# A three-layer chain on one core: the first stage of an f32 kernel in another written order

## The chip, the core and the metric

The kernel runs on one core of a Trainium2 chip. A core has five engines that work side by side, each through a list of its own: TensorE (PE, matmuls), VectorE (DVE), ScalarE (ACT), GpSimd (POOL) and SyncE (SP, which here issues the DMAs). The metric is the device time of one execution in microseconds, and lower is better.

## What is computed

Chunked attention, then a gated layer behind an RMS norm, then a layer with a cosine gate, all in float32. The reference, cut to its core:

```python
# attention: 8 batches x 8 heads, 576 positions in chunks of 64, head size 64
scores = (1 / sqrt(64)) * q_c @ k_c.T
attn = exp(scores - max(scores));  attn = attn / (sum(attn) + 1e-9)
x = (attn @ v_c) as 4608 tokens x 512
# gated layer, 512 -> 1536 -> 512
xn = x / sqrt(mean(x * x) + 1e-6) * rms_g
x = (silu(xn @ w_gate) * (xn @ w_val)) @ w_out
# cosine layer, 512 -> 2048 -> 512
h = x @ w_in
out = (h * cos(h)) @ w_out2
```

Each float32 factor of the large products is split into two parts of fewer bits, and three matmuls (high by high, high by low, low by high) are added in PSUM.

## The kernel before

The program has four stages. This text is about the first, which ends some 303 us into the span. It does three jobs at once.

**Attention.** The 4608 tokens are 36 units of 128, handled in 18 pairs. For a unit `n` (or pair `u`) the steps have one letter each: `Q` and `V` load q, k and v; `s` multiplies q by k for a pair (L418, for the first pair L401); `m` takes the row maximum on DVE (L435); `b` subtracts it on DVE (L450); `e` is the exponential on ACT (L454); `n` sums on DVE, inverts and scales the row (L459 to L469; for the first two units the scaling is a step `z` of POOL); `t` transposes on PE (L476) and `c` copies the result out on ACT (L481); `v` multiplies by v for a pair (L492); `r` squares and sums on ACT (L506), `w` makes the norm's factor on POOL, `y` applies it on DVE (L517); `x` transposes on PE (L525); `j` rounds the high part on ACT (L534), `a` keeps a full copy on ACT (L539), and `l` makes the low part on DVE (L547; for the first two units on POOL, L545). `X` stores the copy.

**A first third of the gated layer.** Four of the twelve column blocks of `w_gate` and `w_val` are multiplied here in the plain way. The weights of block `f`, matrix `m` (0 gate, 1 value) are loaded by `Dfm` and split by `k`, `p`, `q`, `H`, `L` (ACT, DVE, DVE, ACT, POOL). The tokens go in eleven chunks, `A` to `D` of 256 columns and `E` to `K` of 512. `gA0` is the gate product of chunk A with block 0, 12 matmuls into one PSUM bank, `vA0` the value product; `SA0` is the SiLU on ACT (L594), which empties the gate's bank; `hA0` multiplies the two on DVE (L604), and `Y` stores.

**Preparation of later weights.** Steps `Pl0` to `Pk15` load, split and store sixteen blocks of weights for the second stage.

The gate and value products share a ring of four PSUM banks with the scores of pairs 1 and 3; the other four banks serve scores, transposes and outputs of the attention in turn.

What sets the order: every step is written once in one long table, `ORDER`, and each engine takes its instructions strictly in the order in which the table's steps issue them.

```python
with tc.manual_schedule(engines=FIXED):   # PE, DVE, ACT, POOL, SP
    for name in ORDER.split():
        ...
        step(name)
```

A second table, `ORDER2`, does the same for stages two and three. The steps `O1` and `O2` in the first table already make operands of the second stage, which begins with products named `b` (L293, with 384 columns). Its high parts are casts at L352, its low parts subtractions at L357.

Of the kernel before, what the change touches and what calls it, by code (L numbers as in the profile page):

```python
# [82 lines left out]
def kernel(  # L83
# [58 lines left out]
    a4 = {n: [("op4", n, k) for k in range(2)] for n in range(EARLY4)}  # L142
# [216 lines left out]
    with ExitStack() as st:  # L359
# [290 lines left out]
        def step(name):  # L650
# [16 lines left out]
                units[kind](int(n))  # L667

        ORDER = """
            D00 Q0 k00 Q1 Q2 p00 s0 q00 Q3 H00 I m0 b0 D01 V0 V1 sx m1 Pl0 Dg b1 e0 n0 Q4 e1 L00 z0 s1 n1 t0 m2 b2 Q5 z1 m3  # L670
            t1 V2 b3 e2 c0 c1 k01 e3 v0 n2 n3 t2 r0 t3 Pa0 p01 V3 Pb0 w0 r1 c2 y0 w1 y1 D20 Q6 q01 x0 s2 j0 a0 H01 V4 c3 Pc0
            m4 m5 b4 b5 Pd0 x1 e4 j1 v1 l0 Q7 n4 e5 k20 r2 n5 D21 a1 w2 t4 V5 V6 p20 r3 t5 Pl1 c5 y2 w3 y3 q20 s3 x2 k21 D11
            c4 l1 x3 j2 H20 p21 Q8 v2 m7 m6 gA0 j3 L20 D10 X0 L01 l3 l2 a2 r4 a3 gB0 Pa1 b6 b7 Q9 vA0 q21 e7 n7 vB0 X1 e6 n6
            w4 r5 SA0 w5 t7 H21 k11 SB0 c7 L21 D30 gA2 y4 y5 x4 t6 Pb1 j4 k10 x5 hA0 hB0 l4 a4 a5 p10 j5 Pc1 l5 gB2 s4 V7
            SA2 vA2 vB2 gC2 Ph0 Q10 SB2 Pl2 m9 m8 k30 hA2 b8 Po0 q10 b9 p11 c6 e8 n8 Q11 v3 e9 r7 D31 hB2 n9 p30 q11 gC0 H10
            vC2 t8 SC2 SC0 r6 vC0 w7 L10 YA0 w6 gB1 y7 YB0 YA2 gA1 t9 y6 s5 c8 hC2 hC0 H11 V8 x6 k31 q30 c9 L11 SB1 V9 H30
            Pa2 Q12 X2 vB1 m10 m11 V10 L30 b10 Pk0 vA1 Q13 YB2 YC2 V11 j6 b11 x7 SA1 YC0 v4 a6 p31 Q14 e11 gC1 hA1 Pl3 r9
            e10 q31 r8 H31 hB1 l6 n11 j7 gA3 w9 Pd1 vC1 gB3 w8 L31 n10 a7 SC1 l7 t10 y8 t11 c11 c10 SA3 Ph1 vA3 X3 y9 s6 hC1
            Pb2 x8 Pc2 Po1 x9 SB3 vB3 m12 b12 Q15 Pl4 V12 e12 m13 hA3 b13 hB3 gC3 e13 n12 Pk1 YA1 Pd2 j8 v5 a8 j9 gD1 V13
            Q16 YB1 r10 a9 r11 gD0 l8 V14 t12 SD1 X4 w10 YA3 vD1 n13 l9 y10 c12 x10 SC3 w11 Ph2 t13 y11 hD1 s7 m15 m14 SD0  # L680
            j10 a10 b14 vD0 vC3 c13 l10 e14 x11 v6 gD3 b15 hD0 Q17 gD2 V15 YC1 e15 Po2 r12 a11 Pa4 j11 n14 hC3 n15 w12 Q18
            l11 vD3 r13 w13 t14 SD3 c14 y12 Pb4 y13 vD2 t15 V16 Pc4 s8 x12 c15 SD2 m16 Pa3 j12 x13 m17 b16 gE0 b17 e16 a12
            v7 Q19 vE0 e17 hD3 Pd4 hD2 l12 n16 r14 gE1 Pk2 n17 j13 r15 t16 V17 w15 X5 w14 y15 a13 Ph4 y14 SE0 l13 t17 c17
            Pb3 c16 s9 Po4 m18 b18 gE2 x15 e18 m19 x14 b19 e19 j14 Pc3 Pd3 j15 n19 v8 hE0 r17 a14 V18 X6 w17 SE1 r16 y17 vE1
            vE2 YC3 a15 l15 w16 n18 Pk4 Q20 Q21 hE1 Pl5 Ph3 gE3 y16 t19 V19 l14 V20 Pa5 SE3 c19 SE2 t18 Pb5 s10 m20 X7 hE2
            x16 vE3 Pc5 b20 c18 Po3 m21 b21 x17 gF2 e20 Q22 Pk3 v9 Pd5 Ph5 e21 a16 Pl6 gF0 j16 j17 Po5 n20 r18 l16 r19 n21
            t20 vF0 l17 a17 Pa6 W8 w19 Q23 V21 t21 Pl7 w18 hE3 y19 V22 c20 y18 s11 x18 c21 m22 SF2 SF0 m23 Q24 vF2 Q25 b22
            b23 Pb6 a18 YE1 hF2 Pc6 Pk5 e22 gF3 x19 Pa7 j18 v10 Q26 Pl8 Q27 V23 e23 V24 Pd6 Ph6 YE3 j19 r20 r21 hF0 gF1 n23
            Pb7 w20 l18 Po6 w21 Pc7 SF3 Pa8 SF1 n22 y20 vF3 a19 l19 vF1 t23 c23 t22 y21 Pd7 s12 m25 x20 Pk6 X8 Ph7 c22 a20
            Po7 m24 gG0 b24 x21 b25 j20 a21 e25 Pb8 hF3 v11 e24 r22 j21 V25 Pl9 r23 X9 vG0 Pc8 w23 Pk7 Pa9 n24 hF1 gG2 SG0  # L690
            Pd8 Ph8 y23 Q28 l20 l21 gG1 n25 Pl10 w22 V26 hG0 y22 V27 t24 vG2 YF3 Po8 t25 s13 Pb9 SG2 SG1 Pa10 c24 m27 m26
            b26 YD3 x22 W9 b27 Pc9 c25 j22 a22 Pb10 gG3 Pk8 x23 v12 Pd9 j23 r25 e27 e26 hG2 l23 r24 a23 Pc10 l22 n26 vG1 vG3
            W10 gH2 X10 w24 Q29 w25 SG3 Ph9 Pl11 Po9 Pl12 YF1 n27 W11 y25 t26 c26 t27 y24 s14 hG1 hG3 m28 c27 Pa12 Pb12 b28
            SH2 Q30 YG1 x24 m29 j24 Pd10 e28 gH3 x25 l24 b29 e29 j25 Pk9 V28 Q31 vH2 l25 a24 n28 v13 Q32 YB3 V29 X11 a25 SH3
            r27 r26 w27 w26 Pc12 hH2 n29 gH0 t28 vH3 t29 SH0 Ph10 Po10 c28 Pa11 c29 V30 Q33 y26 y27 s15 x26 gH1 m30 b30 x27
            Pb11 m31 Pk10 hH3 Pc11 b31 a26 j26 j27 vH0 e30 YH3 W12 Pd12 Pl13 YG3 l26 v14 l27 hH0 X12 V31 n30 e31 gI0 r28 r29
            vH1 SH1 Ph12 w28 w29 Po12 n31 t31 y29 a27 Q34 t30 y28 c31 SI0 Pa13 s16 m32 m33 b32 x28 gI2 b33 hH1 Q35 Pk12 Pd11
            c30 W13 x29 j28 SI2 l28 Pb13 gI1 e33 Ph11 Pl14 j29 v15 X13 vI0 Po11 n33 l29 hI0 Pc13 r30 e32 Pk11 r31 a28 SI1
            vI2 Pa14 Pl15 V32 n32 V33 a29 X14 w30 Pd13 t33 gI3 t32 c33 Ph13 c32 YD1 w31 hI2 y30 Pb14 Po13 y31 x30 vI1 Pc14
            s17 hI1 x31 W14 Pk13 V34 vI3 j30 a30 SI3 j31 m34 l30 b34 l31 W19 m35 b35 Pd14 v16 Pa15 hI3 r33 Ph14 gJ2 r32 Po14  # L700
            YD0 W20 YD2 V35 e34 a31 X15 e35 w32 Pb15 W21 Pc15 gJ3 Pk14 SJ2 vJ2 y32 n35 n34 gJ0 t35 t34 Pd15 w33 YH1 y33 c35
            c34 x32 x33 vJ0 SJ3 j32 v17 Ph15 a32 j33 a33 X16 r35 r34 Po15 l32 w34 YI3 w35 vJ3 YI1 hJ2 Pk15 gJ1 hJ3 y34 SJ0
            l33 x34 y35 SJ1 hJ0 j34 x35 j35 a34 vJ1 l35 l34 gK2 gK0 hJ1 a35 X17 Z W15 W16 SK0 SK2 YJ3 vK2 gK1 gK3 W17 W18
            vK0 O1 hK2 hK0 SK3 SK1 vK1 O2 vK3 hK3 hK1 YJ1 YK3 YK1
            """
        nc.gpsimd.memset(mhalf, -0.5)
        nc.gpsimd.memset(halfpi, math.pi / 2)
# [234 lines left out]
    def saved(acc, tag):  # L942
        t = pools["left3"].tile([P, 2, H], F32, tag=tag, name=tag)
        nc.scalar.copy(t, acc)  # L944
        return t
# [248 lines left out]
    with fourth:  # L1194
        for s in range(FIRST, NB):
            for g in range(G3):
                z = {"b1": opened("b1", 2)}
                multiply(z["b1"], s, 1, g, True)
                z1 = saved(z["b1"], "z1")
# [160 lines left out]
```

## Time and profile before

| | |
|---|---|
| time, median of 3 runs | 1626.80 us (1626.78 to 1627.53) |
| the profiled execution | 1626.93 us, of which the span of the program is 1625.1 us |
| PE busy | 1603.0 us, 99% of the span |
| DVE busy | 1362.6 us, 84% |
| ACT busy | 953.4 us, 59% |
| POOL busy | 237.4 us, 15% |

The span is the time from the first to the last instruction on the chip; the 1.8 us between it and the time of that execution lie around it. A matmul's recorded duration is longer than its distance from the next one, since matmuls overlap in the array. So the pace of PE is read from starts of groups, not from durations, and short pauses do not show as idle time. In lists of what the program issues, one f32 matmul of 64 rows stands once (x32), and in the trace it is two passes (x64).

### The profile page before, as it was taken

The numbers are of one execution on the slowest core, as the hardware profiler recorded it, in microseconds if no ns is written. First come the engines' busy times: TensorE is split into PE (matmuls) and PEld (weight loads), VectorE is DVE, ScalarE is ACT, GpSimd is POOL, SyncE is SP. The second block draws the span as 40 slices with busy tenths as digits, with TensorE's granted clock in tenths as the row PEclk, the third lists the DMA queues.
The fourth block names the chain that finished last, engine by engine and source line by source line (L and its number), as shares of the span: only waits on it lengthen the run. The fifth ranks groups of instructions, "written<-read, shape, count | busy, mean of one in ns | idle before, by whom it ended". The sixth has DMA issues, their size and how long they took to land.

```text
span 1625.1 us, 29201 instructions
## 1 busy us (share of the span) xinstructions
PE 1603.0 (99%) x11208; PEld 1556.7 (96%) x11208; DVE 1362.6 (84%) x1862; ACT 953.4 (59%) x1378; POOL 237.4 (15%) x276
## 2 busy tenths in 40 slices
PE   6999999999999999999999999999999999999998
PEld 5998888899999999999999999999999999999998
DVE  7988776588988886889999689988989977877876
ACT  4877665354655544445555478887888634444443
POOL 3434434022223221001112000000000000000000
PEclk9999999999999999999999999999999999999999
DMA  8778988797767778786677864433433665346331
GB/s 294 249 252 277 315 284 270 267 329 247 238 220 250 246 228 272 288 260 201 204 250 243 303 250 145 147 133 130 146 123 120 230 211 163 100 126 185 106 100 39
DMA packets 293131, 342.98 MB, mean 211 GB/s; under 512 B 87936, under 2 KB 265600, under 8 KB 292992
## 3 DMA queue, kind: packets, MB, share of 16 engines
q1 hardware_dynamic: 292192, 341.02, 64.5%
q8 instruction: 88, 1.44, 0.4%
q14 instruction: 51, 0.42, 0.1%
q10 hardware_dynamic: 800, 0.10, 0.0%
HBM read 197.92 MB, written 143.13 MB: 210 GB/s over the span
## 4 chain that ended last, share of the span: by engine, by line
PE 92%; DVE 5%; issue 1%; DMA 0%; ACT 0%; POOL 0%; SPq 0%; DVEq 0%; ACTq 0%; POOLq 0%
PE b L293 76%; PE g L293 6%; PE v L293 6%; PE o L492 1%; PE sc L418 1%; PE tr L525 1%; PE pt L476 1%; DVE xt L357 1%; DVE z L808 1%; DVE wraw L198 0%; DVE z L819 0%; DVE wt L127 0%; DVE wt L128 0%; DMA raw<-in_w_dram 0%; DVE q L339 0%
## 5 line engine op out<-in xcount | busy, mean ns | idle before, releaser
L293 PE MATMUL b<-xo,w 128*128 128x384 f32 x3528 | 612.9, 334 | 0.0
L293 PEld LDWEIGHTS b<-xo,w 128*128 128x128 f32 x3528 | 611.4, 188 | 1.2 <-ACT xo L280 0.7
L293 PE MATMUL b<-xt,w 128*128 128x384 f32 x1728 | 305.9, 335 | 2.4 <-ACT z L804 0.9
L293 PEld LDWEIGHTS b<-xt,w 128*128 128x128 f32 x1728 | 299.6, 188 | 5.2 <-ACT z L804 2.0
L293 PE MATMUL b<-x,w 128*128 128x384 f32 x1440 | 261.9, 334 | 0.2 <-DVE z L808 0.2
L293 PEld LDWEIGHTS b<-x,w 128*128 128x128 f32 x1440 | 250.3, 188 | 1.4 <-DVE z L808 0.6
L280 ACT CAST xo<-q 128x768 fp32r<-128x768 f32 x144 | 118.3, 836 | 117.6 <-PE b L293 97.7
L281 DVE TENSOR_TENSOR xo<-q,xo 128x768 fp32r<-128x768 f32 x144 | 135.2, 953 | 53.2 <-ACT xo L280 53.1
L293 PE MATMUL b<-q,w 128*128 128x384 f32 x864 | 157.7, 334 | 0.0
L293 PEld LDWEIGHTS b<-q,w 128*128 128x128 f32 x864 | 150.5, 188 | 0.0
L251 POOL TENSOR_TENSOR wout<-wt,wout 128x384 fp32r<-128x384 f32 x44 | 54.6, 1242 | 433.2 <-ACT wout L249 330.2
L861 ACT CAST xo<-rawh 128x768 fp32r<-128x768 f32 x98 | 79.7, 836 | 57.6 <-PE b L293 27.8
L804 ACT COPY z<-b 128x768 f32<-128x768 f32 x72 | 57.3, 798 | 88.6 <-PE b L293 64.8
L293 PE MATMUL v<-xt,w 128*128 128x512 f32 (+1 forms) x528 | 107.6, 356 | 0.0
L293 PE MATMUL g<-xt,w 128*128 128x512 f32 (+1 forms) x528 | 107.6, 355 | 0.0
L866 DVE TENSOR_TENSOR xo<-rawh,xo 128x768 fp32r<-128x768 f32 x98 | 96.0, 1013 | 3.2 <-ACT xo L861 3.1
L293 PEld LDWEIGHTS g<-xt,w 128*128 128x128 f32 x528 | 85.7, 189 | 13.3
L293 PEld LDWEIGHTS v<-xt,w 128*128 128x128 f32 x528 | 85.6, 189 | 13.0
L808 DVE TENSOR_TENSOR z<-b,z 128x768 f32<-128x768 f32 x72 | 68.3, 952 | 31.6 <-PE b L293 20.4
L949 DVE TENSOR_TENSOR u<-b,z 128x768 f32<-128x768 f32 x72 | 68.2, 952 | 15.6 <-ACT z L944 12.7
L969 DVE SCALAR_TENSOR_TENSOR q<-q,u 128x768 f32<-128x768 f32 x72 | 68.5, 952 | 10.7 <-ACT q L967 10.2
L959 DVE SCALAR_TENSOR_TENSOR q<-q,u 128x768 f32<-128x768 int32 x72 | 68.2, 952 | 10.0 <-ACT q L955 9.7
(139 smaller groups left out, 2068.2 us busy)
## 6 DMA issues: line engine op xcount, KB each, us to landing
wraw<-in_w_dram SPq DMA_DIRECT2D x240, 128.0 KB, 3.4
gd<-q SPq DMA_DIRECT2D x80, 384.0 KB, 2.5
q<-gd SPq DMA_DIRECT2D x80, 384.0 KB, 3.9
rawh<-hd SPq DMA_DIRECT2D x66, 384.0 KB, 5.4
w<-kout SPq DMA_DIRECT2D x49, 512.0 KB, 7.0
qk<-in_qk_dram SPq DMA_DIRECT2D x36, 512.0 KB, 6.2
kgv<-wout SPq DMA_DIRECT2D x16, 896.0 KB, 6.5
w<-kgv SPq DMA_DIRECT2D x28, 512.0 KB, 6.7
```

The lines of the kernel that those rows point to most:

```text
L251: nc.gpsimd.tensor_tensor(b[n][:, :, 1], a, f32(b[n][:, :, 0]), op=ALU.subtract)
L280: nc.scalar.copy(hi, a)
L281: nc.vector.tensor_tensor(lo, a, f32(hi), op=ALU.subtract)
L293: nc.tensor.matmul(acc, a, b, start=first and k == 0 and q == 0, stop=k == n - 1 and q == 2, skip_group_check=True)
L357: nc.vector.tensor_tensor(o[:, 1], sourceg(s, j), f32(o[:, 0]), op=ALU.subtract)
L804: nc.scalar.copy(sums[s, g, k], z[s, g, "b1"])
L808: nc.vector.tensor_tensor(t, z[s, g, "b2" if k == 0 else "b5"], t, op=ALU.add)
L861: nc.scalar.copy(to[0], source2(s, g, j))
L866: nc.vector.tensor_tensor(to[1], source2(s, g, j), f32(to[0]), op=ALU.subtract)
L949: nc.vector.tensor_tensor(t, acc, part, op=ALU.add)
L959: nc.vector.scalar_tensor_tensor(q, k, -1.0, u, op0=ALU.mult, op1=ALU.add)
L969: nc.vector.scalar_tensor_tensor(q, q, -PI2, u, op0=ALU.add, op1=ALU.mult)
```

## The change

One literal is replaced: the table `ORDER` of the first stage. It has the same steps, each once, in another order; nothing else in the file differs. The steps of one chain keep their order among themselves. Its first two lines were and are:

```diff
         ORDER = """
-            D00 Q0 k00 Q1 Q2 p00 s0 q00 Q3 H00 I m0 b0 D01 V0 V1 sx m1 Pl0 Dg b1 e0 n0 Q4 e1 L00 z0 s1 n1 t0 m2 b2 Q5 z1 m3
-            t1 V2 b3 e2 c0 c1 k01 e3 v0 n2 n3 t2 r0 t3 Pa0 p01 V3 Pb0 w0 r1 c2 y0 w1 y1 D20 Q6 q01 x0 s2 j0 a0 H01 V4 c3 Pc0
...
+            D00 Q0 Q1 k00 Q2 p00 q00 s0 m0 I Q3 b0 e0 sx m1 b1 e1 Pl0 V0 n0 n1 z0 V1 H00 s1 z1 t0 m2 t1 b2 m3 c0 e2 b3 D01
+            Q4 c1 n2 Dg Pa0 Q5 e3 k01 L00 v0 t2 r0 V2 n3 Pb0 p01 r1 c2 w0 y0 t3 w1 c3 y1 x0 s2 V3 q01 Q6 j0 D20 a0 Pc0 m4 m5
...
```

Through the transposes `x2 x3` of pair 1 PE's list does not change. The first difference on PE is what follows them. Before, from those transposes on (`o` is step `v2`, `pt` are `t6 t7`, `tr` are first `x2 x3`, then `x4`; the 256-column products are `gA0 gB0`, `vA0 vB0`, `gA2`):

```order
L525 MATMUL tr<-ident,xn 128x128 x8
L492 MATMUL o<-v,pts 64x64 x32
L293 MATMUL g<-xt,w 128x256 x24
L293 MATMUL v<-xt,w 128x256 x24
L476 MATMUL pt<-ident,p 128x128 x4
L293 MATMUL g<-xt,w 128x256 x12
L525 MATMUL tr<-ident,xn 128x128 x4
```

In the changed table, at the same place (products `gA0`, then `gB0 vA0 gA2 vB0`):

```order
L525 MATMUL tr<-ident,xn 128x128 x8
L293 MATMUL g<-xt,w 128x256 x12
L492 MATMUL o<-v,pts 64x64 x32
L293 MATMUL g<-xt,w 128x256 x12
L293 MATMUL v<-xt,w 128x256 x12
L293 MATMUL g<-xt,w 128x256 x12
L293 MATMUL v<-xt,w 128x256 x12
L476 MATMUL pt<-ident,p 128x128 x8
L525 MATMUL tr<-ident,xn 128x128 x4
```

`gA0` now stands ahead of `v2`, `gA2` ahead of `vB0`, and both transposes `t6 t7` ahead of `x4`.

On DVE the list is the same up to here but for one swap of two weight conversions. Then, before (`mx` are `m6 m7`, `xt` are `l2 l3`, `p` are `b6 b7`):

```order
L123 TENSOR_SCALAR t<-t 128x512
L435 TENSOR_REDUCE mx<-sc 128x8 x2
L547 TENSOR_TENSOR xt<-tr,xt 128x4x128 x2
L450 TENSOR_TENSOR p<-sc,mx 128x512 x2
L127 SCALAR_TENSOR_TENSOR t<-raw,t 128x512
```

and in the changed table:

```order
L123 TENSOR_SCALAR t<-t 128x512
L435 TENSOR_REDUCE mx<-sc 128x8
L547 TENSOR_TENSOR xt<-tr,xt 128x4x128 x2
L435 TENSOR_REDUCE mx<-sc 128x8
L450 TENSOR_TENSOR p<-sc,mx 128x512 x2
L127 SCALAR_TENSOR_TENSOR t<-raw,t 128x512
```

The second maximum has moved behind the two low parts.

On ACT the stretch that ends with the first SiLU reads, before (`xf` is step `a`, `xn` step `r`, `p` are `e6 e7`):

```order
L539 COPY xf<-tr 128x4x128
L506 ACTIVATE xn,ss<-o 128x512
L539 COPY xf<-tr 128x4x128
L119 ACTIVATE wt<-wraw 128x512
L454 ACTIVATE p<-p 128x512 x2
L506 ACTIVATE xn,ss<-o 128x512
L594 ACT_TABLE_LOAD
L594 ACTIVATE sg<-g 128x256
```

and in the changed table:

```order
L570 CAST w<-t 128x512
L506 ACTIVATE xn,ss<-o 128x512
L454 ACTIVATE p<-p 128x512 x2
L506 ACTIVATE xn,ss<-o 128x512
L594 ACT_TABLE_LOAD
L594 ACTIVATE sg<-g 128x256 x2
```

The cast of weights (`H01`) has come in from further up, the copy `a3` and the conversion of raw weights have gone further down, and `SA0 SB0` follow each other.

## Rows read from the trace of the kernel before

**Rows 1.** The page: busy time, share of the span and instructions of each engine.

```profile
PE 1603.0 (99%) x11208; PEld 1556.7 (96%) x11208; DVE 1362.6 (84%) x1862; ACT 953.4 (59%) x1378; POOL 237.4 (15%) x276
```

**Rows 2.** PE's waits, whole run: total us, times, longest.

```profile
PE sc L401 <- DMA qk<-in_qk_dram: 6.1, 1, 6.1
PE pt L476 <- DVE p L469: 2.4, 3, 1.5
...
PE o L492 <- issue: 1.4, 2, 0.8
```

**Rows 3.** Windows: length, busy PE, PEld, DVE, ACT, POOL, clock granted, DMA, GB/s.

```profile
25.00:30.00 5.00, 3.28 (x100) 2.60 (x95) 4.70 (x10) 3.14 (x8) 2.97 (x5) 1.00 0.46 143
30.00:32.00 2.00, 1.09 (x4) 0.72 (x4) 1.90 (x5) 1.72 (x6) 0.93 (x3) 0.53 0.92 252
32.00:34.00 2.00, 1.66 (x28) 1.36 (x32) 1.97 (x5) 0.49 (x2) 1.92 (x3) 0.50 0.92 217
34.00:36.00 2.00, 2.00 (x56) 1.88 (x49) 1.93 (x4) 1.16 (x3) 0.18 (x1) 0.50 1.01 344
36.00:38.00 2.00, 2.00 (x54) 1.66 (x53) 1.62 (x3) 1.58 (x3) 0.40 (x1) 0.76 0.96 293
...
240.00:280.00 40.00, 40.00 (x373) 33.14 (x372) 26.07 (x44) 22.70 (x43) 17.45 (x28) 1.00 0.82 270
```

**Rows 4.** The chain in order of time, 31 to 39 us: start, us, what.

```profile
31.50 0.70 DVE p L469
...
37.16 0.86 PE o L492 x48
38.02 0.63 issue
```

**Rows 5.** Timeline of PE, 37 to 48 and 268 to 283 us: start, us, group.

```profile
37.09 0.93 PE L492 MATMUL o<-v,pts 64*64 64x64 f32 x48
...
39.04 3.14 PE L293 MATMUL g<-xt,w 128*128 128x256 f32 x24
...
44.91 0.60 PE L476 MATMUL pt<-ident,p 128*128 128x128 f32 x4
45.26 1.67 PE L293 MATMUL g<-xt,w 128*128 128x256 f32 x12
46.77 0.60 PE L525 MATMUL tr<-ident,xn 128*128 128x128 f32 x4
...
271.23 1.16 PE L492 MATMUL o<-v,pts 64*64 64x64 f32 x64
272.33 3.02 PE L293 MATMUL v<-xt,w 128*128 128x512 f32 x12
```

**Rows 6.** The page: the queue that carries instructions, packets, MB, share.

```profile
q8 instruction: 88, 1.44, 0.4%
```

**Rows 7.** Timeline of DVE and ACT, 38 to 46 us.

```profile
38.04 1.29 DVE L547 TENSOR_TENSOR xt<-tr,xt 128x512 fp32r<-128x512 f32 x2 [0.42 <-ACT xt L534]
...
39.25 1.27 DVE L450 TENSOR_TENSOR p<-sc,mx 128x512 f32<-128x512 f32 x2
...
41.47 1.14 ACT L454 ACTIVATE p<-p 128x512 f32<-128x512 f32 x2
...
43.21 1.28 ACT L594 ACT_TABLE_LOAD   x1
44.51 0.39 ACT L594 ACTIVATE sg<-g 128x256 f32<-128x256 f32 x1
...
45.69 1.40 DVE L517 SCALAR_TENSOR_TENSOR xn<-o,rs,gamma 128x512 f32<-128x512 f32 x2
```

**Rows 8.** Timeline at the start of the second stage, PE and ACT.

```profile
303.28 6.86 PE L293 MATMUL b<-xt,w 128*128 128x384 f32 x37
303.48 1.57 ACT L352 CAST xt<-q 128x768 fp32r<-128x768 f32 x2 [3.40 <-PE v L293]
...
310.69 2.53 PE L293 MATMUL b<-xt,w 128*128 128x384 f32 x13 [0.55 <-DVE xt L357]
```

More of the change, by code (lines that the diff above doesn't have):

```diff
@@ L669 @@
         ORDER = """
-            D00 Q0 k00 Q1 Q2 p00 s0 q00 Q3 H00 I m0 b0 D01 V0 V1 sx m1 Pl0 Dg b1 e0 n0 Q4 e1 L00 z0 s1 n1 t0 m2 b2 Q5 z1 m3
-            t1 V2 b3 e2 c0 c1 k01 e3 v0 n2 n3 t2 r0 t3 Pa0 p01 V3 Pb0 w0 r1 c2 y0 w1 y1 D20 Q6 q01 x0 s2 j0 a0 H01 V4 c3 Pc0
-            m4 m5 b4 b5 Pd0 x1 e4 j1 v1 l0 Q7 n4 e5 k20 r2 n5 D21 a1 w2 t4 V5 V6 p20 r3 t5 Pl1 c5 y2 w3 y3 q20 s3 x2 k21 D11
-            c4 l1 x3 j2 H20 p21 Q8 v2 m7 m6 gA0 j3 L20 D10 X0 L01 l3 l2 a2 r4 a3 gB0 Pa1 b6 b7 Q9 vA0 q21 e7 n7 vB0 X1 e6 n6
@@ L674 @@
[L674 to L702, printed above, removed]
@@ L703 @@
-            l33 x34 y35 SJ1 hJ0 j34 x35 j35 a34 vJ1 l35 l34 gK2 gK0 hJ1 a35 X17 Z W15 W16 SK0 SK2 YJ3 vK2 gK1 gK3 W17 W18
-            vK0 O1 hK2 hK0 SK3 SK1 vK1 O2 vK3 hK3 hK1 YJ1 YK3 YK1
+            D00 Q0 Q1 k00 Q2 p00 q00 s0 m0 I Q3 b0 e0 sx m1 b1 e1 Pl0 V0 n0 n1 z0 V1 H00 s1 z1 t0 m2 t1 b2 m3 c0 e2 b3 D01
+            Q4 c1 n2 Dg Pa0 Q5 e3 k01 L00 v0 t2 r0 V2 n3 Pb0 p01 r1 c2 w0 y0 t3 w1 c3 y1 x0 s2 V3 q01 Q6 j0 D20 a0 Pc0 m4 m5
+            Q7 b4 x1 Pd0 j1 b5 l0 D21 e4 v1 n4 e5 a1 r3 n5 t4 r2 t5 k20 s3 w2 V4 c4 p20 V5 c5 y2 w3 y3 D10 Pl1 Q8 V6 q20 x2
@@ new lines @@
+            k21 H20 l1 j2 x3 j3 p21 a2 m6 l2 gA0 v2 l3 m7 D11 H01 b6 b7 r5 L20 Q9 e6 e7 r4 gB0 SA0 q21 L01 n6 SB0 w4 a3 n7
+            vA0 gA2 vB0 Pa1 y4 t6 t7 x4 w5 H21 L21 V7 gB2 X0 D30 hA0 c6 hB0 y5 s4 Pb1 V8 j4 k10 c7 p10 k11 SA2 Pc1 x5 Q10 m8
+            l4 b8 Ph0 j5 SB2 vA2 a4 vB2 l5 Po0 YA0 D31 k30 v3 e8 hB2 hA2 m9 q10 p11 b9 r6 V9 H10 Pl2 YB0 Q11 X1 V10 gC2 gC0
+            e9 V11 vC2 Q12 SC2 vC0 k31 SC0 a5 Pa2 n8 n9 L10 w6 YB2 YA2 r7 q11 hC2 p30 gB1 hC0 t9 w7 H11 c9 y6 y7 gA1 YC2 X2
@@ new lines @@
+            Q13 gC1 t8 p31 s5 x6 q30 Pk0 SA1 L11 vA1 c8 H30 SB1 Q14 j6 q31 x7 m11 hA1 m10 vC1 vB1 H31 j7 b10 a6 a7 b11 L30
+            l7 SC1 e10 v4 L31 hB1 Q15 e11 hC1 l6 n10 gA3 Pl3 gB3 r9 V12 Pd1 r8 SB3 SA3 n11 w8 Pb2 w9 vA3 vB3 y8 y9 hA3 t11
+            t10 s6 hB3 Pc2 m12 c11 x8 Ph1 c10 j8 b12 a8 gD1 x9 m13 b13 l8 e12 e13 j9 vD1 v5 r10 Po1 SD1 gC3 gD0 Q16 Pd2 Pl4
+            YA1 YC0 r11 n12 w10 n13 t13 Pk1 X3 w11 y10 l9 c13 a9 YB1 V13 y11 hD1 vD0 t12 Pa4 SD0 c12 Ph2 s7 SC3 x10 j10 x11
+            vC3 Q17 j11 Pb4 m14 m15 b14 YC1 b15 YA3 gD3 V14 v6 e14 a10 l10 gD2 hD0 l11 hC3 a11 vD3 e15 r12 r13 w12 n14 vD2
@@ new lines @@
+            X4 w13 Q18 n15 t14 t15 SD2 y13 y12 Po2 SD3 Q19 V15 Pa3 Pc4 s8 m16 b16 c14 m17 V16 c15 b17 e16 gE0 x12 Pk2 x13
+            j12 hD2 hD3 n16 l12 v7 j13 r14 w14 e17 gE1 n17 V17 a12 r15 w15 vE0 l13 y14 y15 a13 t17 Pb3 SE0 SE1 Pd4 c17 t16
+            s9 m18 m19 b18 c16 x14 Ph4 j14 vE1 x15 b19 Pc3 e19 v8 Q20 r17 r16 Q21 V18 Po4 n19 V19 X5 hE0 X6 a14 j15 gE2 l14
+            Pk4 Pd3 e18 gE3 hE1 t19 Pl5 w16 vE2 y16 Pa5 w17 c19 a15 n18 V20 Ph3 l15 Pb5 y17 t18 s10 SE2 Q22 x16 SE3 c18 m20
+            b20 Po3 vE3 x17 Pc5 hE2 Q23 m21 e20 b21 j16 j17 a16 Pd5 Pl6 n20 l16 gF2 X7 V21 v9 Pk3 Ph5 Pa6 Pl7 Q24 r18 hE3
@@ new lines @@
+            l17 YC3 YE1 vF2 gF0 t20 e21 n21 V22 Q25 W8 r19 Po5 w19 SF2 Pk5 a17 w18 Pb6 y19 c20 Pa7 y18 t21 s11 m22 c21 x19
+            vF0 hF2 x18 V23 Pc6 Pd6 m23 gF3 j18 b22 b23 v10 SF0 e23 Ph6 e22 Pl8 X8 a18 r20 gF1 Q26 SF3 Pb7 j19 Q27 w20 Po6
+            Pc7 Pl9 Pk6 hF0 vF3 r21 a19 n23 YE3 SF1 Pa8 n22 l19 hF3 l18 w21 Pd7 vF1 t23 y20 Ph7 y21 t22 Pb8 s12 V24 YF3 X9
+            m24 b24 Po7 hF1 m25 b25 c22 c23 gG0 e24 gG2 x20 n24 Pc8 e25 x21 v11 Pa9 n25 j20 j21 YD3 a20 a21 SG2 Pk7 V25 Pd8
+            Q28 Pl10 W9 r22 vG0 vG2 r23 SG0 Ph8 l21 l20 Pb9 w23 t24 Pc9 y23 hG2 hG0 w22 Po8 t25 y22 Pl11 gG1 s13 c24 SG1 c25
@@ new lines @@
+            x23 x22 m26 V26 X10 V27 j22 b26 m27 gG3 b27 j23 Pa10 v12 e27 a22 e26 vG1 r25 a23 l23 Pk8 Pb10 l22 Q29 Pc10 n26
+            Pd9 r24 n27 w24 hG1 YF1 SG3 w25 y24 Q30 Pl12 V28 y25 gH2 vG3 t26 t27 Ph9 c26 s14 Po9 Pd10 x24 j24 vH2 gH3 Q31
+            m28 b28 m29 Pk9 Pa12 c27 a24 b29 e28 SH2 e29 l24 Pb12 V29 YG1 x25 W10 Pc12 hG3 n28 Q32 j25 v13 r27 X11 Q33 r26
+            Ph10 w26 W11 V30 n29 hH2 w27 a25 y26 vH3 t28 gH0 l25 y27 Po10 c28 t29 SH3 s15 m30 hH3 x27 c29 m31 Pk10 b30 W12
+            b31 x26 gH1 v14 SH0 Pa11 j26 j27 vH0 a26 Pb11 a27 e30 l27 l26 r29 Pd12 r28 w28 e31 YG3 Pc11 w29 SH1 Ph12 W13
@@ new lines @@
+            Pl13 V31 X12 n30 y29 Po12 Pk12 YB3 gI0 n31 t30 vH1 Pl14 V32 t31 y28 s16 m33 m32 Q34 Pd11 hH0 b32 c30 c31 SI0
+            Pa13 x28 vI0 b33 x29 e33 Ph11 hI0 Po11 gI2 v15 hH1 Pb13 gI1 vI2 Pc13 n33 gI3 e32 Pa14 j28 r30 Pd13 a28 j29 r31
+            a29 X14 w31 w30 YH3 n32 Pb14 l29 l28 X13 SI2 YH1 t33 y30 Q35 t32 Pk11 y31 hI2 x30 vI1 j30 c32 c33 Ph13 s17 V33
+            W14 Pc14 l30 m34 Pl15 YD2 b34 m35 Po13 x31 SI1 j31 SI3 a30 Pa15 a31 X15 vI3 V34 W19 YD1 Pk13 v16 hI1 r33 l31
+            Pd14 Pb15 b35 Pc15 r32 e34 w32 YI1 Ph14 gJ2 gJ3 SJ2 vJ2 n34 y32 hI3 Po14 Pk14 x32 t34 gJ0 V35 e35 w33 n35 a32
@@ L705 @@
+            y33 j32 SJ3 Pd15 Ph15 t35 l32 hJ2 Po15 YD0 YI3 W20 x33 c34 c35 a33 X16 vJ0 v17 SJ0 r35 vJ3 r34 w35 j33 w34 gJ1
+            y35 hJ3 l33 y34 x34 x35 j34 hJ0 vJ1 Pk15 W21 a34 l34 j35 a35 X17 l35 Z W15 W16 gK2 gK0 SJ1 hJ1 SK0 SK2 gK3 YJ3
+            vK2 vK0 W17 W18 hK0 hK2 SK3 gK1 O1 vK3 O2 SK1 vK1 hK3 YK3 hK1 YJ1 YK1
             """
```

## The prediction

> **What bounds the kernel now.** I read the busy time first. PE is busy for 1603.0 of 1625.1 us and no other engine for more than 84% of the span [rows 1]. A change that neither removes nor adds a matmul can then give back at most the time in which PE stands still or runs slowly, 1625.1 - 1603.0 = 22 us in all. So the question is where PE stands still, and whether the first stage's new order touches those places.
>
> The list of PE's waits answers half of it. The longest is the first load (6.1 us for q and k); then come transposes that wait for the scaled rows of DVE (2.4 us in three waits), and 1.4 us in two pauses for which the profile names nothing but issue [rows 2]. All of these lie ahead of 39 us. From 39.04 us on, the groups of PE follow each other until the products of the second stage begin at 303.28 us [rows 5, 8]: in the ten windows that I read from 40 to 280 us, of which the last is shown, PE is busy for the whole length of each [rows 3].
>
> The windows show the stretch before that. From 25 to 36 us DVE is busy for 4.70 of 5 us, then 1.90 of 2, 1.97 of 2 and 1.93 of 2, while PE has holes (3.28 of 5, 1.09 of 2, 1.66 of 2) and TensorE's clock stands at half, 1.2 GHz, from 30 us on; it is back at full in the course of 36 to 38 us [rows 3]. So DVE sets the pace of the start. The chain in order of time says when that ends: its last piece on DVE there is the scaling of a row at 31.50 us, and from then on it stays on PE, up to a piece of 0.63 us at 38.02 us that is neither work nor a wait, but issue [rows 4].
>
> That piece is the one hole after PE has become what limits. It lies inside `v2`, which is one group of 64 passes: 48 of them start at 37.09 us, 16 more only after the pause, and the next group begins at 39.04 us, 39.04 - 37.09 = 1.95 us after its start. The same group of pair 17 takes 272.33 - 271.23 = 1.10 us [rows 5]. So `v2` loses 1.95 - 1.10 = 0.85 us there (0.63 shows as idle, the rest is covered by recorded durations). All its operands were used by the first 48 passes too, so a late operand can't be the reason; I take it that PE ran out of instructions. The queue that carries instructions moved 1.44 MB in 88 packets, 16.4 KB each [rows 6], and PE has 2 x 11208 matmuls and weight loads [rows 1], 255 for each packet if they are PE's. Around 33 to 38 us PE works through two groups of 64 tiny passes each (`s3`, `v2`) with only eight transposes between them, faster than anywhere else.
>
> **The change, part by part.**
>
> *Ahead of `x2 x3` (37.1 us).* The lists of PE and DVE are the same but for one swap of two conversions on DVE. What moves are casts and exponentials on ACT, two products of POOL and loads on SP. ACT is busy for 3.14 of 5 us from 25 to 30 us and DVE for 4.70 [rows 3], so a shift of ACT inside its own idle time gives nothing as long as DVE's list is unchanged: the last DVE piece stays at 31.50 us [rows 4]. The cover is DVE's own work; without it, an exponential moved ahead by one cast would give 0.6 us. Terms: 0, with bounds from -0.6 to +0.6 us by that same cast's length (1.14 / 2 = 0.57 us for one of a pair of ACT's full-width steps [rows 7]).
>
> *`gA0` ahead of `v2`.* Twelve matmuls of some 1.5 us (the group of twelve at 45.26 us takes 46.77 - 45.26 = 1.51 us [rows 5]) go between `x2 x3` and `v2`. Their operands are there: the tokens of units 0 and 1 and the weights of block 0 are among the first that were split. PE then needs 1.51 us longer to reach the place in its list where it paused, longer than the pause of 0.85 us, so that what it waited for has come. I book the pause as gone: -0.85 us. The bounds are 0 (the pause stays) and -0.85 us (it can't give more than it took).
>
> *`m7` behind `l2 l3` on DVE.* DVE stood for 0.42 us ahead of the low parts, waiting for ACT [rows 7]. With one maximum behind them instead of ahead, `l2` comes earlier and the wait has work in it: DVE gains up to 0.42 us on its list. PE does not wait for it there, so this gives nothing itself, but it is the slack that the next point needs.
>
> *`gA2` ahead of `vB0`, `t7` ahead of `x4`.* Two places get tighter. `vB0` is now the fifth product since the scores of pair 3, and its bank is the one that `gA0` filled, so it waits for `SA0` on ACT. On PE it starts at 44.91 (its end before) - 0.85 + 1.51 - 1.5 = 44.1 us. On ACT `r5` can begin when `v2` ends, 37.09 + 1.51 + 1.10 = 39.7 us; then an estimated 0.7 for `r5` (0.57 for a full-width step, half of the 1.14 of `e6 e7`, and a little to read out the sum), 1.14 for `e6 e7`, 0.7 for `r4`, 1.28 for the table and 0.39 for `SA0` [rows 7]: 43.9 us, 0.2 us ahead. `x4` comes at 46.77 - 0.85 + 0.35 (a transpose of four, 45.26 - 44.91) = 46.3 us [rows 5]. Its input `y4` ends at 45.69 + 0.70 = 46.4 us on DVE before, and up to 0.42 us sooner now [rows 7]. Terms: 0 each, with bounds of +0.1 us for `x4` and, for `vB0`, up to one table load, +1.3 us.
>
> *The rest of the stage.* The number of groups on PE stays nearly the same (two fewer rows), and every group of 64 passes still stands alone. So I book 0. ACT switches its table oftener, 34 loads in the program's list instead of 30, which is 4 x 1.28 = 5 us [rows 7] on an engine with 41% of the span idle [rows 1].
>
> *The handover.* The second stage's first wait, 0.55 us at 310.69 us, comes from a chain that starts when the last product of the first stage releases a tile: two casts on ACT at 303.48 us, after 3.40 us of waiting for PE [rows 8], then low parts on DVE. In the new order one of two gate multiplications moves out of DVE's way there, but DVE waits for those casts anyway. Term 0, bound -0.55 us.
>
> The sum, against the profiled execution's own time: 1626.93 - 0.85 = **1626.1 us**. That execution stands 0.13 us above the median of the runs, so this is 0.05% less than either. A difference of 0.2%, 3.25 us, is about what a measurement can tell from no change.
>
> **The rivals.**
>
> *The gain does not come.* Either the pause is tied to the place in the list rather than to PE's pace, or `x4` and `vB0` hand it to DVE and ACT. For it: DVE is nearly full all through the start [rows 3], and a PE that runs 0.85 us ahead runs into it. Against it: the margins of 0.2 us and of up to 0.3 us worked out above. Time: 1626.9 us. The Trainium skill speaks for the first form: "Runtime: NRT & Kernel Launch", section "Instruction fetch mechanics", says that instructions come in blocks of 16 KiB or 256 and that crossing into a block is mostly hidden. The size agrees with 16.4 KB and 255; if the hiding held here too, the pause would have another cause and stay, and the time would be 1626.9 us.
>
> *Slower: `vB0` waits for its bank, and the clock falls.* Place: PE at 44 us. It decides once `SA0` is over 1 us late, that is, if ACT's row of `r5 e6 e7 r4` and the table load slips that much behind; then PE stands about as much as from 25 to 30 us (1.7 of 5 us), after which the clock fell to half [rows 3]. At half clock from 30 to 36 us PE was busy for 1.09 + 1.66 + 2.00 = 4.75 us [rows 3], work of 2.4 us at full clock. Price: 1 + 2.4 = 3.4 us or more, time 1629.5 us and up to 1631 us. Against it: no row of before shows ACT that late.
>
> *Faster: the clock comes back sooner.* If the half-clock stretch from 30 to 37 us were gone, those 4.75 us would be 2.4, and the time 1626.1 - 2.4 = 1623.7 us. Against it: PE's holes there come from DVE's unchanged list, so nothing in the change fills them.
>
> **How the numbers follow.** I give the forecast 0.58 (its own range 1625.5 to 1626.5 us, by the bounds of the start and of `x4`), no gain 0.24, slower with the clock 0.08, faster with the clock 0.06, and 0.04 to a wait later in the stage that I did not find, on the slow side. The time is that of the forecast, 1626.1 us. The range leaves out the two clock cases and that last one: from 1624.8 us (forecast less 0.6 for the start and 0.55 for the handover, and a little) to 1628.2 us (no gain, and one slip of ACT by a table load's 1.3 us). Only the outer parts of the clock cases pass 0.2%: faster 0.04, slower 0.07, no difference 0.89.
>
> **What would show it.** Right: `v2` is one group of 1.1 us with no pause of issue, `gA0` stands before it at 37.1 us, the products of the second stage begin at about 303.28 - 0.85 = 302.4 us, and the first wait there is still about 0.55 us. Wrong: a wait of PE between 39 us and the second stage, above all at `vB0` for `sg` or at `x4` for `xn`; a pause of issue elsewhere; or a half-clock stretch that is longer or shorter than from 30 to 37 us.

## The result, and the profile after

The new order takes 1641.9 us (median of four runs, 1640.75 to 1642.14) against 1627.16 us, a ratio of 1.0089 with a 95% interval of 1.0077 to 1.0102. The forecast was 1626.1 us in a range of 1624.8 to 1628.2: it missed by 15.8 us, on the other side.

The page first, busy time, share and instructions of each engine [rows 1]; the span is 1640.3 us:

```profile
PE 1608.3 (98%) x11208; PEld 1559.3 (95%) x11208; DVE 1362.9 (83%) x1862; ACT 959.0 (58%) x1382; POOL 237.5 (14%) x276
```

The span grew by 15.2 us, PE's busy time by only 5.3, part of it the same matmuls at a lower clock. PE has to have stood still. The timeline says up to where: start, length and group of PE at the start of the second stage [rows 8].

```profile
318.14 6.86 PE L293 MATMUL b<-xt,w 128*128 128x384 f32 x37
325.55 0.62 PE L293 MATMUL b<-xt,w 128*128 128x384 f32 x2 [0.55 <-DVE xt L357]
```

The first product of the second stage starts at 318.14 instead of 303.28 us, 14.86 us late. Nearly all of the loss is in the first stage, and the handover's wait of 0.55 us is as it was. PE's waits between 60 and 300 us (us in total, times, longest) name no place in which the trace of before had any wait at all [rows 2, 3]:

```profile
PE pt L476 <- DVE p L469: 3.1, 1, 3.1
PE g L293 <- DVE xt L547: 2.4, 2, 1.6
PE o L492 <- ACT xf L539: 1.7, 1, 1.7
PE sc L418 <- ACT pts L481: 1.0, 1, 1.0
PE tr L525 <- DVE xn L517: 0.8, 1, 0.8
PE sc L418 <- DMA qk<-in_qk_dram: 0.8, 1, 0.8
PE sc L418 <- issue: 0.6, 1, 0.6
```

They add up to 10.4 us. Four of them stand alone, at 104, 134, 194 and 202 us. The rest come close together, and the windows show what that costs besides [rows 3]:

```profile
240.00:280.00 40.00, 33.59 (x325) 27.00 (x324) 21.17 (x39) 20.82 (x38) 16.09 (x26) 0.96 0.67 215
280.00:285.00 5.00, 4.27 (x16) 3.59 (x17) 2.44 (x4) 4.54 (x8) 2.25 (x2) 0.66 0.99 330
```

PE was busy for all of 240 to 285 us before, at a clock of 1.00, and is now for 33.59 of 40 and 4.27 of 5; right behind its waits the granted clock falls to half (means of 0.96 and 0.66). The group of 23 products that starts at 264.48 us takes 6.70 us up to the start of the next group; 24 of them take 5.60 at full clock (in `e2b_one_store`, from 261.03 us). By the two means the clock stands at half for 0.04 x 40 x 2 + 0.34 x 5 x 2 = 6.6 us, which costs by estimate up to 3.3 us; with the waits that makes 13.7 of the 14.86 us.

PE waits for ACT and DVE here, so the question is what they wait for. The timeline of ACT in the same stretch (only the two lines with a long wait for a DMA):

```profile
258.29 0.51 ACT L636 CAST wout<-wt 128x384 fp32r<-128x384 f32 x1 [5.67 <-DMA kgv<-wout]
...
273.81 0.51 ACT L636 CAST wout<-wt 128x384 fp32r<-128x384 f32 x1 [7.00 <-DMA kgv<-wout]
```

ACT's waits for this tile from 200 to 300 us, in total, times and longest, before and after:

```profile
ACT wout L636 <- DMA kgv<-wout: 0.4, 1, 0.4
ACT wout L636 <- DMA kgv<-wout: 12.7, 2, 7.0
```

L636 is the step `Ph`: it casts a weight of the second stage into the tile `wout`, which has one buffer. It may write there only when the step `Pk` of the weight before has stored the tile in memory, and that store is issued by SP. So twice ACT stands for 5.67 and 7.00 us, not for work but for a store, and everything behind it on its list stands too: the copies that free PE's PSUM banks, SiLU, the next exponentials (DVE waits 8.57 us for one of them). The queue of SP shows why the store is late:

```profile
235.06 0.43 SPq L374 DMA_DIRECT2D qk<-in_qk_dram  x1
244.61 0.52 SPq L551 DMA_DIRECT2D xd<-xf  x1
245.18 0.63 SPq L608 DMA_DIRECT2D hd<-h  x1
245.85 1.01 SPq L551 DMA_DIRECT2D xd<-xf  x1
246.95 1.25 SPq L608 DMA_DIRECT2D hd<-h  x1
248.25 1.22 SPq L374 DMA_DIRECT2D qk<-in_qk_dram  x1
249.57 1.23 SPq L204 DMA_DIRECT2D kgv<-wout  x1
```

SP takes its list in order. At 235.5 us it comes to `X14`, a store of token rows that ACT copies last at 243.97 us, and waits nine microseconds. Behind it stand, after three more stores, the load `Q35` and the store `Pk11` (the last two lines), whose tile POOL had ready at 242.5 us. The second wait comes about in the same way: the tile for `Pk13` is ready at 261.10 us, and the store, behind `X15`, is issued at 266.58. The five stores of `wout` from 225 to 290 us take 4.9 to 8.6 us from issue to landing, which ACT waits for as well. In the old order `Q35` and `Pk11` stood ahead of `X14`:

```profile
225.31 1.02 SPq L374 DMA_DIRECT2D qk<-in_qk_dram  x2
...
238.68 0.52 SPq L204 DMA_DIRECT2D kgv<-wout  x1
...
246.28 0.56 SPq L551 DMA_DIRECT2D xd<-xf  x1
```

SP waited for ACT's copies there too (8.7 us in two waits from 200 to 290 us, now 14.1), but no store behind those waits kept ACT waiting for more than 0.4 us.

At the start, where the prediction looked, this is PE's timeline [rows 5]:

```profile
35.88 1.68 PE L293 MATMUL g<-xt,w 128*128 128x256 f32 x12
37.48 0.80 PE L492 MATMUL o<-v,pts 64*64 64x64 f32 x37
39.05 0.68 PE L492 MATMUL o<-v,pts 64*64 64x64 f32 x27 [0.76 <-issue]
39.66 1.69 PE L293 MATMUL g<-xt,w 128*128 128x256 f32 x12
```

`gA0` (35.88 us) is now ahead of `v2`, and the pause is still there, 11 passes earlier in `v2`. The tight places `vB0` and `x4` do not wait here.

### The profile page after: what moved, and what is told of

Same layout as the page of the kernel before. It is cut to its first block, busy times and chain, and to the rows that moved or that the text cites. A ratio compares the mean times of both kernels' runs of the same rounds, so it can differ in the third digit from the quotient of the medians.

```text
span 1640.3 us, 29206 instructions
## 1 busy us (share of the span) xinstructions
PE 1608.3 (98%) x11208; PEld 1559.3 (95%) x11208; DVE 1362.9 (83%) x1862; ACT 959.0 (58%) x1382; POOL 237.5 (14%) x276
## 4 chain that ended last, share of the span: by engine, by line
PE 72%; DVE 2%; issue 0%; DMA 0%; SPq 0%; ACT 0%; DVEq 0%; ACTq 0%
PE b L293 72%; DVE z L808 0%; DMA q<-xd 0%; DVE xt L357 0%; DVE wraw L198 0%; DVE z L819 0%; DVE q L339 0%; DVE wt L127 0%; DVE sg L819 0%; ACT z L804 0%; DMA out_dram<-o 0%; DVE wt L128 0%; SPq L827 0%; DVE wt L123 0%; SPq L1247 0%
```

## Experiments

**The theory** was the one just read: stores that SP issues behind an `xd` store hold ACT through the single `wout` buffer. **Its rivals**: the four table loads that ACT has more (34 in the list instead of 30); lateness handed on from the middle of the stage; the late load `Q35`. Each run below is given with the median of the kernel before on the same chip.

### Where the loss sits: three mixed orders

Each takes one order up to a step and then the other order for the steps that are left.

```diff
-ORDER = new
+h1_new_head:   ORDER = new up to SA2 (50 us), then old without the steps already there
+h2_new_to_s15: ORDER = new up to s15 (222 us), then old
+h3_old_to_s15: ORDER = old up to s15, then new
```

> The new order up to SA2 (about 50 us), from there the old one for what is left. If the loss comes only later, as the two traces say, this is as fast as before or up to 0.6 us faster: 1626.2 to 1627.0 us. If the new head already puts ACT behind so that the old rest stumbles over it, over 1629 us.

> The new order up to the scores s15 (about 222 us), then the old order for the rest. By the two traces the waits up to there (at 104, 134, 194 and 202 us) cost 4.0 us: theory of the tail expects 1627 - 0.6 + 4 = 1630.5 us, span of the first stage about 306.5 to 307.5 us at the first product of the second stage, and no wait of ACT for a stored wout of over 1 us behind 225 us. The rival that lateness is handed on from the new middle to the tail expects 1636 us or more.

> The old order up to s15, then the new one for the rest. Theory of the tail: the weight stores Pk11 and Pk13 again stand behind xd stores, ACT waits twice for a stored wout (5 us or more each), and the time is 1627 + 11 = 1638 us. Rival (ACT is late because of the new middle): 1630 us or less.

Measured: 1627.32 us for the new head (ratio 1.0003, 0.9994 to 1.0012), 1631.48 us for the new order up to `s15` (1.0029, 1.0018 to 1.0040), 1638.17 us for the new tail alone (1.0069, 1.0054 to 1.0084), before 1626.91. So the head costs nothing, the middle 4.6 us, the tail 11.3; the two make 15.9, somewhat more than the loss of 14.7. The tail needs no lateness from the middle: in `h3_old_to_s15` ACT's timeline has the two waits again.

```profile
254.22 0.51 ACT L636 CAST wout<-wt 128x384 fp32r<-128x384 f32 x1 [5.81 <-DMA kgv<-wout]
...
269.95 0.52 ACT L636 CAST wout<-wt 128x384 fp32r<-128x384 f32 x1 [6.99 <-DMA kgv<-wout]
```

And with the old tail behind the new middle (`h2_new_to_s15`) ACT has no wait for a stored `wout` from 200 to 303 us, and PE's waits from 60 to 300 us are those of the middle alone, 3.3 us in all; the other 1.3 of the 4.6 us stand in no wait that the profile lists:

```profile
PE sc L418 <- ACT pts L481: 1.0, 1, 1.0
PE tr L525 <- DVE xn L517: 0.9, 1, 0.9
PE g L293 <- DVE xt L547: 0.8, 1, 0.8
PE sc L418 <- issue: 0.6, 1, 0.6
```

### Taking the cause away: three DMA steps, and one alone

```diff
 ... s16 m33 m32 Q34
+Q35                      # e2
 Pd11 hH0 ... Ph11 hI0 Po11
+Pk11                     # e2 and e2b
 gI2 v15 ... a29 X14 ... y30
-Q35                      # e2
 t32
-Pk11                     # e2 and e2b
 y31 ... m35 Po13
+Pk13                     # e2
 x31 ... X15 vI3 V34 W19 YD1
-Pk13                     # e2
 v16
```

> The new order with three steps moved that only SP carries out: Q35 right behind Q34, Pk11 right behind Po11, Pk13 right behind Po13, each ahead of the xd store that it stood behind. Theory of the stores: ACT's two waits for a stored wout (5.67 and 7.00 us) fall below 1 us each, and 6 to 9 us of the 15 come back: 1633 to 1636 us. Rival (four more table loads make ACT late): ACT is late all the same, and no more than 2 us come back, 1640 us.

> The new order with one step moved: Pk11, the store of a split weight, right behind Po11 and so ahead of the xd store X14. Theory of the stores: ACT's first wait for a stored wout (5.67 us at 258.29) goes, the second (7.00 us, Pk13 behind X15) stays at 5 us or more, and PE's two waits around 260 us (1.71 and 1.58 us, with the half clock behind them) go, while the wait of a transpose for p around 277 us stays: 4 to 6 us come back, 1636 to 1638 us. If instead the late qk load Q35 started it all, nothing comes back: 1641 us.

All three moved: 1631.25 us (1.0031, 1.0019 to 1.0042), 10.65 us of the 14.7 back (10.4 with each kernel against its own median of before), more than expected. No instruction of PE, DVE, ACT or POOL changed its place. ACT's waits from 200 to 300 us begin with PE and no longer contain `wout`:

```profile
ACT xt L534 <- PE tr L525: 13.4, 5, 4.6
ACT pts L481 <- PE pt L476: 9.2, 4, 4.8
```

`Pk11` alone: 1639.49 us (1.0074, 1.0059 to 1.0089; before 1626.95), only 2.4 us back where 4 to 6 were expected. ACT's first wait went and the second stayed (6.16 us). PE's two waits around 260 us went too, but the other two grew, since PE now ran into them sooner:

```profile
255.51 1.15 PE L418 MATMUL sc<-qk 64*64 64x64 f32 x60 [1.55 <-DMA qk<-in_qk_dram]
277.48 0.77 PE L476 MATMUL pt<-ident,p 128*128 128x128 f32 x4 [4.35 <-DVE p L469]
```

So the 10.65 us are not a sum with one term for each step: a wait removed is partly paid at the next one. How they divide between `Q35` and `Pk13` no run separates. PE's own wait for the load of `Q35` is 0.8 us in the new order and 1.55 us here, so the load has a share of its own beside the stores.

### Putting the cause into the old order

```diff
 ... Po11 n33 l29 hI0 Pc13 r30 e32
-Pk11
 r31 a28 ... a29 X14
+Pk11
 w30 Pd13 t33
```

> The old order with one step moved the other way: Pk11 right behind X14, an xd store that SP issued at 260.92 us. Theory of the stores: the store then lands at about 266 us instead of about 256, ACT's cast for Ph13 (256.86 us, 0.37 us of waiting for the store) waits about 9 us, everything behind it on ACT is late, and PE loses 4 to 10 us: 1631 to 1637 us. Rival (the old order's ACT, with four table loads less, has the room): under 1629 us.

One step, 1632.91 us (1.0035, 1.0023 to 1.0047; before 1626.95): 6.0 us slower, within what the theory expected, with the old order's 30 table loads. The expectation had the pair one round too late in time: `X14` is the `xd` store that before issues at 246.28 us, and the cast that waits is the one that ran at 244.71 us. ACT and PE show the chain:

```profile
253.62 0.51 ACT L636 CAST wout<-wt 128x384 fp32r<-128x384 f32 x1 [9.18 <-DMA kgv<-wout]
```

```profile
255.19 1.07 PE L525 MATMUL tr<-ident,xn 128*128 128x128 f32 x4 [4.31 <-ACT pts L481]
255.92 4.30 PE L293 MATMUL v<-xt,w 128*128 128x512 f32 x12
```

A store issued 8 us later (246.58 instead of 238.68) holds ACT for 9.18 us, PE for 4.31, and the twelve products behind run at less than full clock (4.30 us instead of about 3.0).

### What is left: the middle

```diff
 e6 = e2 and, each behind the step that PE waited for:
-Pa3 ... c14 m17 V16 c15        +c14 m17 V16 c15 Pa3
-l15 Pb5 y17                    +l15 y17 Pb5
-l23 Pk8 Pb10 l22               +l23 Pk8 l22 Pb10
-n27 w24 hG1 YF1 SG3 w25 y24    +n27 w24 YF1 SG3 w25 y24 hG1
-a30 Pa15 a31                   +a30 a31 Pa15
 e7 = e6 and:
-l22 Pb10 Q29 Pc10 ... y25      +l22 Q29 ... y25 Pb10 Pc10
```

> The new order with the three steps of SP ahead as in the second run, and at each of the five places where PE still waited there (1.04, 0.72, 0.81, 0.59 and 0.80 us at 104, 134, 194, 201 and 260 us) one step put behind the step that PE waited for: Pa3 behind c15, Pb5 behind y17, Pb10 behind l22, hG1 behind y24, Pa15 behind a31. If the five waits are what is left of the loss, they fall to under 0.2 us in all and 1631.25 - 3.96 = 1627.3 us is measured (1626.5 to 1628). If each hides a next wait, over 1629 us.

> As the run with five swaps, and Pb10 and Pc10 (four conversions of a weight on DVE) behind y25 instead of ahead of n26, since in that run a transpose still waited 0.89 us at 199 us for DVE's p, late behind those four. From the place behind v2 to the second stage's first wait that run took 312.37 - 40.28 = 272.1 us. Theory: under 271.3 us, no wait of PE over 0.2 us from 60 us on, and 1628.98 - 0.9 = 1628.1 us or, with a head like those of the other runs, down to 1626.5 us. ACT still loads its table 34 times; the rival that these four loads cost the time expects 1630 us or more.

`e6_five_swaps` takes 1628.98 us (1.0010, 1.0001 to 1.0020; before 1626.95), with the 34 table loads of the new order: these loads can have cost no more than a part of the 2.0 us that are left. Of the five waits of `e2_stores_ahead` all are gone and one came new, the single line of PE's waits from 60 to 300 us:

```profile
PE pt L476 <- DVE p L469: 0.9, 1, 0.9
```

1627.3 us was expected, so 1.7 us were missed: 0.9 is that new wait, which I had not foreseen: PE comes sooner to a transpose whose `p` stands on DVE behind four conversions of a weight. `e7_six_swaps`, meant to remove it, failed: 1631.83 us (1.0030, 1.0019 to 1.0041; before 1627.22). The wait at 199 us went, and another came ten microseconds on. First PE, then ACT:

```profile
209.46 4.56 PE L293 MATMUL v<-xt,w 128*128 128x512 f32 x12 [2.48 <-DVE h L604]
```

```profile
204.21 0.66 ACT L119 ACTIVATE wt<-wraw 128x512 f32<-128x512 f32 x1 [3.62 <-DMA wraw<-in_w_dram]
```

`Pc10` is the last reader of a `wraw` buffer. Moved back, it released the buffer later, the next load into it was issued at 200.44 us instead of 194.60, and ACT stood 3.62 us for that load. That is the same kind of chain as the stores', made by a step that I had looked at on DVE's list only.

### The pause in `v2`

```diff
 p1:  ... x2 x3
+gA0
 v2 ...
-gA0
 p2, in first_s for unit 0, behind its own products:
+    extra = ps_g.tile([P, D], F32, tag="gv", name="sd").rearrange("p (a b) -> p a b", b=HD)
+    # 32 products of t into extra
 r1, r2: the two kernels unchanged
```

> The old order with the product gA0 alone moved ahead of v2. By the prediction's step the pause inside v2 goes and 0.85 us come back: 1626.1 us. By what the new order's trace shows, the pause stays at the same place of PE's list, 24 instructions later in time and 11 or 12 passes earlier in v2 (after 36 or 37 of 64), unless the packet of instructions lands over 1.4 us before PE gets there: about 0.8 us of pause, 1626.9 us.

> The old order with 32 more small matmuls (64 passes and as many weight loads, 128 instructions on PE, results not used) right behind s0, where PE waits for DVE. If the pause belongs to a place in PE's list, counted in instructions, it moves 64 passes ahead, out of v2 and into the end of s3, and v2 runs in 1.1 us; if it belongs to v2 or to its operands, it stays behind the 48th pass. Time of the first case 1626 to 1627 us.

> The new order unchanged, profiled a second time. If what differs in the first 40 us between the runs so far (PE is through with v2 and gA0 at 38.6 to 40.3 us in kernels whose lists are the same up to there) comes from the execution, the end of v2 is not at 39.66 us again but differs by 0.3 us or more, with a pause of another length, while the waits behind 60 us come again within 0.2 us each.

> The old order unchanged, profiled a second time: likewise another pause than 0.63 us in v2, and from 40 us on no wait of PE over 0.2 us up to the second stage.

`gA0` alone ahead of `v2`: 1626.74 us (0.9998, 0.9989 to 1.0007; before 1626.95), no difference. In its profile the pause is gone and `v2` runs in one piece. But the second profile of the old order, which nothing was done to (1626.98 us), shows no idle time in `v2` either, nor does that of the new (1640.72 us). The old order again:

```profile
36.63 1.67 PE L492 MATMUL o<-v,pts 64*64 64x64 f32 x64
38.23 3.02 PE L293 MATMUL g<-xt,w 128*128 128x256 f32 x23
```

Not all of the loss is gone there: `v2` takes 38.23 - 36.63 = 1.60 us, 0.50 more than the 1.10 of pair 17. TensorE's clock stands at half for a part of it (a mean of 0.69 from 36 to 38 us), and at the place of the pause 0.24 us lie between the starts of two passes, where 0.04 are usual.

Of the eight waits of the new order behind 60 us, expected again within 0.2 us each, six came so in `r1_new_again`; those at 264 and 281 us were shorter, 1.35 instead of 1.58 and 1.71 instead of 3.06 us.

The length of the pause belongs to the execution. In thirteen profiles with one of the two lists of PE up to there, eight have it, 0.17 to 1.04 us long, always at the same place of the list (behind 48 passes of `v2`, or behind 37 with `gA0` ahead), and five show no idle time. What goes with it stands in the packets of the instruction queue. Beside the landing, the start of the last pass ahead of that place and of the first behind it (us):

```
              packet landed   last pass ahead   first pass behind
before            37.51            37.81              38.65
after             37.65            38.07              39.05
e2_stores_ahead   36.67            37.93              37.97
r2_old_again      36.49            37.59              37.84
```

The eight get there at most 1.12 us after the landing (`h3_old_to_s15` 0.39 us before it) and go on 0.87 to 1.50 us after it. Of the five, `r2_old_again` gets there 1.10 us after the landing and loses the 0.24 us above; the other four get there 1.27 us or more after it and lose nothing. So PE very likely runs out of instructions there; a run in which only the packet came sooner or later is missing. With `gA0` ahead five of nine executions stop, without it three of four. `p2_extra_products` (1626.95 us in one run) has no pause in `v2`, nor at the end of `s3`, with packets that start at 29.10 and 37.80 us; since the unchanged kernel can be without one too, it tells nothing apart.

Does an earlier `gA0` help at all? The table compares when `v2` and `gA0` are both done, when the second stage's first product starts, and what lies between (us, from PE's timeline of each run).

```
                 both done   second stage   between
before             40.58        303.28       262.70
r2_old_again       39.77        302.74       262.97
p1_gA0_alone       39.34        302.84       263.50
h1_new_head        39.74        303.04       263.30
after              39.66        318.14       278.48
r1_new_again       40.15        316.73       276.58
h2_new_to_s15      39.29        306.63       267.34
h3_old_to_s15      40.27        312.84       272.57
e2_stores_ahead    38.58        307.56       268.98
e6_five_swaps      40.28        304.96       264.68
```

The head alone differs by up to 1.7 us between kernels with one list of PE up to there (38.58 and 40.28). Part of it is TensorE's clock, which in the windows from 34 to 36 and from 36 to 38 us has means of 0.76 and 1.00 in `e2_stores_ahead` and of 0.50 and 0.58 in `e6_five_swaps`. And where `p1_gA0_alone` is 0.4 to 1.2 us ahead of the old order, it gives 0.5 to 0.8 back before the second stage, part of it in a new wait for SiLU:

```profile
44.55 1.69 PE L293 MATMUL g<-xt,w 128*128 128x256 f32 x12 [0.16 <-ACT sg L594]
```

## Why the prediction was wrong

**"The rest of the stage. ... So I book 0."** This step failed, and it holds nearly all of the 15.8 us. It counted PE's groups, which do stay, and ACT's table loads, priced at 5 us "on an engine with 41% of the span idle"; the loads cost at most a part of the 2.0 us that `e6_five_swaps` leaves. It left out SP's list. The stretch from 240 to 280 us, of which the prediction showed the window [rows 3], was full before because `Q35`, `Pk11` and `Pk13` stood ahead of stores that wait for ACT, and the new table put them behind: 11.3 us by `h3_old_to_s15`. The three steps put ahead again give back 10.65 us in the new order (`e2_stores_ahead`), and `e3_old_late_store` makes 6.0 out of one of them. The 4.6 us of the middle (`h2_new_to_s15`) are for the most part, 3.3 us, waits at four places where one step of another chain stands ahead of the one PE needs: removing them, and one more in the tail, brought `e6_five_swaps` to within 2.0 us of before, 0.9 of which is the wait that came up with them. The other 1.1 us stay open. The table puts 1.4 us of the 2.0 behind the head (264.68 against 263.30 with the new head and the old rest), and the head of that execution is one of the latest.

**"gA0 ahead of v2 ... -0.85 us."** Wrong in its ground. The pause was read from one execution and booked as a property of the kernel; a second profile of the same kernel shows no idle time there, and its time is the same (1626.98 us). That PE lacked instructions fits the landed packets, though no run shows it by itself. That a longer way to the place cures it did not hold: in the new kernel's first profile the same place of the list stops it again, with `gA0` ahead. Instead of the 1.51 us later that the step booked, PE got there only 0.26 us later (38.07 against 37.81), its transposes having run faster in that execution, and the packet landed later too (37.65 against 37.51).

**The tight places.** `x4` was right. `vB0` waited for SiLU as its rival had it, but for only 0.27 us or so in three heads that ran early (`e2b_one_store`, `e2_stores_ahead`, `e7_six_swaps`), far from the 1 us at which the prediction had the clock fall. The new order's wait of 1.04 us at 104 us left the clock at 1.00 (80 to 120 us). **Ahead of `x2 x3`** and **the handover**: right, 0 each; `h1_new_head` measured no difference, and the handover's wait is 0.55 us in every run.

**The rivals.** That the gain does not come is true of the head. The clock that comes back sooner came in part, by luck. The eight transposes `x2 x3` take 1.02 us up to the start of the next group in `after` (34.86 to 35.88 us), 1.82 in before, and 1.62 in `r1_new_again`, the same kernel as `after`; `v2` and `gA0` are done 0.92 us sooner in `after` than in before, not 2.4. The case that came is the one with 0.04, "a wait later in the stage that I did not find, on the slow side". It had no place, no price and too small a chance: the view that would have given it all three, each engine's list against the waits of before on SP and ACT, was read for the first 50 us only.

## What to carry to other kernels

When a table of steps is written anew, read SP's list first: for every DMA ask what it now stands behind, how long that waits in the old trace, and who waits for what the DMA frees. A wait of SP that cost nothing before can cost as soon as a load or a buffer's release is put behind it, and an engine that is idle for 41% of the time is no cover for it, since its list is in order too. And a gap below a microsecond, seen in one profile, wants a second profile of the same kernel before a forecast rests on it.

## What the runs showed of the hardware

PE can stop without a wait that the profile names. Of thirteen executions eight stop at the same place of PE's list, 0.17 to 1.04 us, and go on 0.87 to 1.50 us after a packet of 16.4 KB of instructions has landed; that PE has run out of them is the likely reading. The Trainium skill, "Runtime: NRT & Kernel Launch", section "Instruction fetch mechanics", says that crossing into a block is mostly hidden. The trace agrees from 40 to 280 us, where PE is busy for the whole length of each window [rows 3], and by that reading not for this block, behind a run of very short passes.

DVE's conversions can take longer beside POOL's subtraction of a weight. In `e2_stores_ahead` POOL works at L640 from 130.36 to 132.78 us; the pair of conversions, which took 0.41 and 0.43 us in before with POOL idle, takes

```profile
130.52 1.14 DVE L122 TENSOR_SCALAR wt<-wt 128x512 f32<-128x512 f32 x1
131.69 1.38 DVE L123 TENSOR_SCALAR wt<-wt 128x512 uint32<-128x512 uint32 x1
```

and the transpose behind waits 0.72 us for the scaling that stands after them. In before the two conversions that begin while POOL is at L640 take 1.22 us (at 114.59 us) and 1.11 us (at 246.36 us). Where a step of POOL falls beside which step of DVE is thus a part of the order too.
